# One-slot tiles in strict turn for every ring of a gated recurrence with a feed-forward network

## The chip, the core and the metric

The kernel runs on one core of a Trainium2 chip. The metric is the time of one execution on the device in microseconds (us); lower is better. The core has five engines: PE (TensorE, the matrix engine), DVE (VectorE), ACT (ScalarE), POOL (GpSimd) and SP (SyncE, which here only issues DMAs). Each works through its own queue in order, and semaphores order them against each other. SBUF is the on-chip memory for data, PSUM the memory that PE writes to.

## The reference

A recurrence over time whose decay depends on a gate, and then a network of two products and two more matrix products, for 4 x 5824 = 23296 tokens of 256 channels:

```python
a_base = 1.0 / (1.0 + np.exp(-a_param))
sig_r = 1.0 / (1.0 + np.exp(-r_gate))
sig_i = 1.0 / (1.0 + np.exp(-i_gate))
log_a = 8.0 * sig_r * np.log(np.clip(a_base, 1e-06, 1.0 - 1e-06))[None, None, :]
a_t = np.exp(log_a)
norm = np.sqrt(np.maximum(1.0 - a_t * a_t, 1e-06))
x_gated = norm * sig_i * x
for t in range(S):
    h = a_t[:, t] * h + x_gated[:, t]
    y[:, t] = h
# then, with y as 23296 rows of 256:
a = y @ w1            # 256 -> 1024
b = y @ w2            # 256 -> 1024
h = a * b @ w3        # 1024 -> 1024
out = h @ w_out       # 1024 -> 256
```

## The kernel before

The tokens are cut into 47 chunks: two of 256, 44 of 512 and one of 256. For each chunk the kernel loads the two gates and x (`r`, `i`, `x`), takes tanh of the gates on ACT, multiplies the input gate with x on POOL or DVE, turns both products so that channels lie on partitions (on PE through PSUM for the first chunks, by a transposing DMA later), forms the decay with an exponential (ACT), its square (POOL, ACT or DVE) and its root (ACT), runs the recurrence as a scan on DVE (`h`), and casts it to bf16 (`y`, mostly POOL). PE then multiplies with w1 (`a` steps, tiles `pa`) and w2 (`b` steps, tiles `pb`); ACT or DVE copies `pa` to SBUF (`c` steps, tiles `sa`); DVE multiplies that copy with `pb` (`m` steps, tiles `g_t`); PE multiplies with the product of w3 and w_out (`D` steps, tiles `po`), ACT or DVE copies that to SBUF (`e` steps, tiles `ot`), and SP stores it (`o` steps). The product of w3 and w_out is formed once in the first 50 us (`Ft`, `Fc`, `Fm`, `Fe` steps, after the loads `L` and casts `C` of the weights).

The order of the work is written out by hand: the string ORDER is a list of some two thousand words, one a step, and the scheduler keeps that order on every engine (`tc.manual_schedule()`, L76; the loop at L570 to L572). In a word the first number is the chunk. `a0.3.1` is the product with w1 for chunk 0, pair 3, half 1; `c0.3.1` is the copy of its result; `b1.2` is the product with w2 for chunk 1, pair 2; `m1.2` multiplies the two; `V4` turns the recurrence gate of chunk 4 and `U4` its gated input; `d4.0` is the decay of chunk 4 for the first half of the channels, `h` the scan, `y` the cast. `W` steps are matmuls without use that keep PE busy in the first microseconds.

Tiles come from pools. A pool with `bufs=N` has N slots for each tag (or as many as the call's own `bufs` says), and tiles of one tag share them. When the program is compiled, each tile is given one of the slots of its tag that are free at that point of the scheduler's own order of events; the choice is then fixed in the program as an address. At run time the first instruction that writes a tile waits, by semaphore, for the last instruction that used the tile before it in the same slot. That wait is in the engine's queue, and what stands behind it in the queue waits too. I call the first write of a new tile a take, and the end of the last use of a tile its release.

The rings are: in PSUM `po` (4 slots of one bank, shared by the tiles `pa`, `po`, `ptr`, `ptw` and `pw`) and `pb` (2 slots of two banks, shared by `pb`, the warm-up tiles and one small one); in SBUF `r` 4, `i` 5, `x` 4, `th_r` 2, `u` 2, `rt` 2, `ut` 6, `a` 6, `nrm` 6 (the last two shared with the staged weights), `h` 2, `y` 4, `sa` 3, `g` 3, `ot` 3, `w3` 4 and `w3t` 2. In the compiled program before, 499 tiles go through the `po` ring and 188 through `sa`.

The lines of the pools are L55 to L62; every helper that takes a tile does so in one line, such as L264 in `up_a` or L281 in `copy`. The instructions of matmuls with w1 and w2 all stand at L260, of `D` steps at L299, copies at L274 (DVE) and L276 (ACT), casts of `y` at L250, scans at L241, products at L288.

Of the kernel before, what the change touches and what calls it, by code (L numbers as in the profile page):

```python
# [22 lines left out]
def kernel(  # L23
# [13 lines left out]
    P = 128  # L37
# [15 lines left out]
    starts = [sum(sizes[:c]) for c in range(NCH)]  # L53

    consts = ctx.enter_context(tc.tile_pool(name="consts", bufs=1))  # L55
    loads = ctx.enter_context(tc.tile_pool(name="loads", bufs=3))
    gates = ctx.enter_context(tc.tile_pool(name="gates", bufs=2))
    held = ctx.enter_context(tc.tile_pool(name="held", bufs=6))
    ypool = ctx.enter_context(tc.tile_pool(name="ypool", bufs=2))
    ffn = ctx.enter_context(tc.tile_pool(name="ffn", bufs=3))  # L60
    psum_b = ctx.enter_context(tc.tile_pool(name="psum_b", bufs=2, space=bass.MemoryType.PSUM))
    psum_o = ctx.enter_context(tc.tile_pool(name="psum_o", bufs=4, space=bass.MemoryType.PSUM))  # L62

    ident_f = consts.tile([P, P], F32, tag="ident_f")
    make_identity(nc, ident_f)
# [29 lines left out]
    FOLD_ACT = {('c', 7), ('e', 0), ('e', 1), ('e', 2), ('e', 3), ('e', 7)}  # L95
    W_ACT = {('w2', 0), ('w3', 6)}
    W_DVE = {('w1', 1)}
    LOAD_BUFS = {"r": 4, "i": 5, "x": 4}
    STAGE = {'w1': ['a', 'a'], 'w2': ['nrm', 'nrm'], 'wo': ['a', 'nrm'], 'w3': ['a', 'nrm', 'a', 'nrm', 'a', 'nrm',
        'a', 'nrm']}  # L100
    CASTING = set()
    WARM = [8, 8, 8, 8, 8, 8, 8, 8, 8, 8, 8, 8, 8, 8, 8, 8]
    src = {"r": rf, "i": jf, "x": xf}

    def flat(t):
# [18 lines left out]

    def load(c, nm):
        n = sizes[c] // P
        t = loads.tile([P, 4, D], F32, name=nm + "_t", tag=nm, bufs=LOAD_BUFS[nm])
        nc.sync.dma_start(  # L128
            out=t[:, :n, :],
            in_=src[nm][starts[c]:starts[c] + sizes[c], :].rearrange("(p n) c -> p n c" if long_rows(c) else "(n p) c -> p n c", p=P))  # L130
        T[nm, c] = t

    def tanh_r(c):
        n = sizes[c] // P
        t = gates.tile([P, NCB, 4, P], BF16, name="th_r", tag="th_r")
        if c in TURN_R:
            nc.scalar.activation(out=flat(t)[:, :n, :], in_=T["r", c][:, :n, :], func=AF.Tanh, scale=0.5)
        else:
            nc.scalar.activation(out=dense(t, n).rearrange("p cb j q -> p j cb q"), in_=cut(T["r", c])[:, :n],  # L139
                                 func=AF.Tanh, scale=0.5)  # L140
        T["thr", c] = t
# [11 lines left out]
    def times(c, half):  # L153
        n = sizes[c] // P
        fused = c in DV_TIMES
        if half == 0 or fused:
            T["u", c] = gates.tile([P, NCB, 4, P], BF16, name="u_t", tag="u")
        u, t, xt = T["u", c], T["thi", c], T["x", c]
        js = slice(0, n) if fused else slice(half * n // 2, (half + 1) * n // 2)
        if c in TURN_U:  # L160
            u, t, xt = flat(u)[:, js, :], t[:, js, :], xt[:, js, :]
        else:
            u, t, xt = dense(u, n).rearrange("p cb j q -> p j cb q")[:, js], cut(t)[:, js], cut(xt)[:, js]
        if fused:
            parts = [slice(None)] if c in TURN_U else [(slice(None), slice(None), cb) for cb in range(NCB)]
            for part in parts:
                nc.vector.scalar_tensor_tensor(out=u[part], in0=t[part], scalar=1.0, in1=xt[part],
                                               op0=ALU.add, op1=ALU.mult)
        else:
            (nc.vector if (c, half) in DV_HALF else nc.gpsimd).tensor_mul(out=u, in0=t, in1=xt)  # L170

    def turn_pe(c, key, nm):
        n = sizes[c] // P
        pt = psum_o.tile([P, NCB, CT], BF16, name="ptr", tag="po")
        for cb in range(NCB):
            for j in range(n):
                nc.tensor.matmul(  # L177
                    out=pt[:, cb, j * P:(j + 1) * P],
                    lhsT=flat(T[nm, c])[:, j, cb * P:(cb + 1) * P], rhs=ident,
                    is_transpose=True,  # L180
                    start=(cb == 0 and j == 0), stop=(cb == NCB - 1 and j == n - 1))
        T[key, c] = pt

    def turn_dma(c, key, nm):
        pool, tag = (gates, "rt") if key == "pr" else (held, "ut")
        dst = pool.tile([P, NCB, 4, P], BF16, name=tag, tag=tag)
        n = sizes[c] // P
        nc.sync.dma_start_transpose(out=dense(dst, n).rearrange("p cb j q -> p (cb j) q"),
                                    in_=dense(T[nm, c], n).rearrange("p cb j q -> p (cb j q)"))
        T[key, c] = dense(dst, n).rearrange("p cb j q -> p cb (j q)")  # L190

    def decay(c, cb):
        w = sizes[c]
        if cb == 0:
            T["a", c] = held.tile([P, NCB, CT], F32, name="a_t", tag="a")
        a, pr = T["a", c][:, cb, :w], T["pr", c][:, cb, :w]
        if long_rows(c):
            a, pr = in_time(a), turned(pr)
        nc.scalar.activation(out=a, in_=pr, func=AF.Exp, scale=la4[:, cb:cb + 1], bias=la4[:, cb:cb + 1])  # L199

    def square(c, cb):
        w = sizes[c]
        if cb == 0:
            T["n", c] = held.tile([P, NCB, CT], F32, name="nrm", tag="nrm")
        n, a = T["n", c][:, cb, :w], T["a", c][:, cb, :w]
        if (c, cb) in AC_SQUARE:
            nc.scalar.activation(out=n, in_=a, func=AF.Square)
# [20 lines left out]
    def scan(c, cb):  # L228
        w = sizes[c]
        if cb == 0:  # L230
            T["h", c] = ypool.tile([P, NCB, CT], F32, name="h_t", tag="h")
        h, a, n = (T[key, c][:, :, :w] for key in "han")
        if cb == 0:
            for b in range(1, B):
# [7 lines left out]

    def cast(c):
        w = sizes[c]
        T["y", c] = ypool.tile([P, NCB, CT], BF16, name="y_t", tag="y", bufs=4)
        if c in AC_CAST:
            nc.scalar.copy(out=T["y", c][:, :, :w], in_=T["h", c][:, :, :w])
        else:
# [1 line left out]
            eng.tensor_copy(out=T["y", c][:, :, :w], in_=T["h", c][:, :, :w])  # L250

    def warm(i):
        pp = psum_b.tile([P, 2, CT], F32, name="warm", tag="pb")
        for _ in range(WARM[i]):
            nc.tensor.matmul(out=pp[:, 0, :P], lhsT=ident, rhs=ident, start=True, stop=True)  # L255

# [4 lines left out]
                             rhs=T["y", c][:, cb, :w], start=(cb == 0), stop=(cb == NCB - 1))  # L261

    def up_a(c, mp, q):
        T["pa", c, mp, q] = pp = psum_o.tile([P, CT], F32, name="pa", tag="po")  # L264
        up(c, 2 * mp + q, pp, w1_sb)

    def up_b(c, mp):
        T["pb", c, mp] = pp = psum_b.tile([P, 2, CT], F32, name="pb", tag="pb")
        for q in range(2):
            up(c, 2 * mp + q, pp[:, q, :], w2_sb)  # L270

# [6 lines left out]
    def copy(c, mp, q):  # L278
        w = sizes[c]
        if q == 0:  # L280
            T["sa", c, mp] = ffn.tile([P, 2, CT], BF16, name="sa", tag="sa")  # L281
        copy_to((c, mp, q) in DV_COPY, T["sa", c, mp][:, q, :w], T["pa", c, mp, q][:, :w])

    def product(c, mp):
        w = sizes[c]
        if mp == 0:
            T["g", c] = ffn.tile([P, KD, CT], BF16, name="g_t", tag="g")
        nc.vector.tensor_mul(out=T["g", c][:, 2 * mp:2 * mp + 2, :w], in0=T["sa", c, mp][:, :, :w],  # L288
                             in1=T["pb", c, mp][:, :, :w])

    def down(c, j):
        if c == NCH - 1:
            T["po_last", j] = po = psum_o.tile([P, D], F32, name="po", tag="po")
        else:
            if j % 2 == 0:
                T["po", c, j // 2] = psum_o.tile([P, 2, D], F32, name="po", tag="po")
            po = T["po", c, j // 2][:, j % 2, :]
        for k in range(KD):
            nc.tensor.matmul(out=po,  # L299
# [1 line left out]
                             start=(k == 0), stop=(k == KD - 1), skip_group_check=True)  # L301

    def evac(c, j2):
        T["ot", c, j2] = ffn.tile([P, 2, D], F32, name="ot", tag="ot")
        copy_to((c, j2) in DV_EVAC, T["ot", c, j2], T["po", c, j2])

    def evac_last(c, j):
        if j % 2 == 0:
            T["ot", c, j // 2] = ffn.tile([P, 2, D], F32, name="ot", tag="ot")
        copy_to(j % 2 == 0, T["ot", c, j // 2][:, j % 2, :], T["po_last", j])  # L310

    def store_last(c, j):
# [24 lines left out]
    def load_w(nm, i):  # L337
        if (nm, i) in CASTING:
            dst = piece(nm, i)[1]
            if dst is None:  # L340
                T["w3b", i] = dst = ffn.tile([P, 1, DFF], BF16, name="w3_t", tag="w3", bufs=4)
            nc.gpsimd.dma_start(out=dst, in_=piece(nm, i)[0])
            return
        T["wf", nm, i] = held.tile([P, NCB, CT], F32, name="wf", tag=STAGE[nm][i])
        nc.sync.dma_start(out=staged(nm, i), in_=piece(nm, i)[0])

    def cast_w(nm, i):
        dst = piece(nm, i)[1]
        if dst is None:
            T["w3b", i] = dst = ffn.tile([P, 1, DFF], BF16, name="w3_t", tag="w3", bufs=4)  # L350
        if (nm, i) in W_ACT:
            nc.scalar.copy(out=dst, in_=staged(nm, i))
        else:
            (nc.vector if (nm, i) in W_DVE else nc.gpsimd).tensor_copy(out=dst, in_=staged(nm, i))

    def fold_t(mi):
        pt = psum_o.tile([P, KD, P], BF16, name="ptw", tag="po")
        for k in range(KD):
            nc.tensor.matmul(out=pt[:, k, :], lhsT=T["w3b", mi][:, 0, k * P:(k + 1) * P], rhs=ident,  # L359
                             is_transpose=True, start=(k == 0), stop=(k == KD - 1))  # L360
        T["ptw", mi] = pt

    def fold_c(mi):
        T["w3t", mi] = ffn.tile([P, KD, P], BF16, name="w3t", tag="w3t", bufs=2)
        copy_to(("c", mi) not in FOLD_ACT, T["w3t", mi], T["ptw", mi])

    def fold_m(mi):
        po = psum_o.tile([P, D], F32, name="pw", tag="po")
        for k in range(KD):
            nc.tensor.matmul(out=po, lhsT=T["w3t", mi][:, k, :], rhs=wo_sb[:, k, :],  # L370
                             start=(k == 0), stop=(k == KD - 1))
# [3 lines left out]
        nc.vector.tensor_copy(out=ident, in_=ident_f)  # L375

    def rates_turn():
        pt = psum_b.tile([P, 2, CT], F32, name="pr_la", tag="pb")
        nc.tensor.matmul(out=pt[:, 0, :NCB], lhsT=la_rows, rhs=ident_f[:NCB, :NCB], is_transpose=True,
                         start=True, stop=True)  # L380
        T["la"] = pt[:, 0, :NCB]
# [219 lines left out]
```

## Time and profile before

| what | value |
|---|---|
| time, median of 3 runs | 519.78 us (519.36 to 521.22) |
| span of the profiled execution | 518.3 us |
| granted clock of TensorE, mean | 0.993 |
| HBM read, written | 78.91 MB, 23.86 MB |
| costliest chain lines | PE L299 28%, PE `pb` L260 28%, PE `pa` L260 27% |

The profile is one execution. Busy shares are of the whole span. "PEclk" is the TensorE clock that was granted, in tenths, in 40 equal slices of the span (13 us each). The chain of waits is followed back from the last instruction; its shares say on which engine the time was spent that set the end. In a timeline a row gives the start in us, the duration in us, the engine, the line, the operation, the tile written and the tiles read, and in brackets how long the engine was idle before it and what ended that. A table of waits gives, for each waiting instruction and each releaser, the total in us, the number of times and the longest.

### The profile page before, as it was taken

The page shows a single profiled execution, that of the slowest core. Times are in us where ns is not written, and L with a number is a line of the kernel's source. Part 1 is how long each engine was busy: PE and PEld are TensorE (multiplying, and loading weights), DVE is VectorE, ACT ScalarE, POOL GpSimd, SP SyncE. Part 2 cuts the span into 40 slices and gives each one's busy share as a digit, 9 for nine tenths or more (in the row PEclk, how much of TensorE's full clock was granted, in tenths as well). Part 3 has the DMA queues.
Part 4 walks back from the last instruction along what each step waited for, and adds up shares of the span by engine and source line. Part 5 has one row for each costly group of instructions (what it writes and reads, how often), then busy time and mean ns, then how long its engine had stood idle before and what let it go on. Part 6 is the DMA issues. An engine that isn't in the chain of part 4 may idle for free.

```text
span 518.3 us, 9099 instructions
## 1 busy us (share of the span) xinstructions
PE 505.2 (97%) x3321; PEld 316.1 (61%) x3321; DVE 428.8 (83%) x414; ACT 466.4 (90%) x720; POOL 314.3 (61%) x271
## 2 busy tenths in 40 slices
PE   7889999999999999999999999999999999999997
PEld 6748665566565566656666656564665665656566
DVE  5869999899899979878879889878888697859762
ACT  7969999999899999999999999998999879888543
POOL 1674657666636975785594985857756659480200
PEclk9979999999999999999999999999999999999999
DMA  8996999989999998998999976989794996352112
GB/s 293 409 414 224 274 341 261 284 260 291 334 232 234 286 266 270 245 214 236 321 296 272 320 231 182 246 224 270 178 277 118 229 290 194 102 144 80 51 62 103
DMA packets 177282, 123.82 MB, mean 239 GB/s; under 512 B 86354, under 2 KB 172884, under 8 KB 177236
## 3 DMA queue, kind: packets, MB, share of 16 engines
q1 hardware_dynamic: 177232, 123.23, 84.2%
q8 instruction: 26, 0.43, 0.3%
q14 instruction: 20, 0.16, 0.1%
q10 hardware_dynamic: 4, 0.00, 0.0%
HBM read 78.91 MB, written 23.86 MB: 198 GB/s over the span
## 4 chain that ended last, share of the span: by engine, by line
PE 85%; DVE 7%; ACT 2%; issue 2%; DMA 2%; SPq 1%; DVEq 0%; ACTq 0%
PE po L299 28%; PE pb L260 28%; PE pa L260 27%; DVE g_t L288 2%; DVE h_t L241 2%; DMA r_t<-in_r_gate_dram 2%; PE pw L370 1%; DVE nrm L224 1%; PE ptr L177 1%; DVE sa L274 1%; PE ptw L359 1%; ACT sa L276 1%; SPq L128 1%; ACT a_t L199 0%; ACT i_t L146 0%
## 5 line engine op out<-in xcount | busy, mean ns | idle before, releaser
L288 DVE TENSOR_TENSOR g_t<-sa,pb 128x1024 bf16<-128x1024 bf16 (+1 forms) x188 | 218.8, 1180 | 65.3 <-PE pb L260 33.0
L260 PEld LDWEIGHTS <-w_sb 128*128 128x128 bf16 x1504 | 147.3, 98 | 150.2 <-issue 9.3
L276 ACT CAST sa<-pa 128x512 bf16<-128x512 f32 (+1 forms) x339 | 182.5, 587 | 29.8 <-PE pa L260 23.2
L260 PE MATMUL pa<-y_t,w_sb 128*128 128x512 bf16 (+1 forms) x752 | 192.2, 374 | 5.8 <-DVE sa L274 4.5
L260 PE MATMUL pb<-y_t,w_sb 128*128 128x512 bf16 (+1 forms) x752 | 185.8, 374 | 0.0
L299 PE MATMUL po<-wp_sb,g_t 128*128 128x256 bf16 x1456 | 177.7, 273 | 0.0
L299 PEld LDWEIGHTS <-g_t 128*128 128x128 bf16 x1456 | 142.4, 98 | 40.0 <-issue 0.2
L250 POOL CAST y_t<-h_t 128x1024 bf16<-128x1024 f32 (+1 forms) x46 | 51.1, 1112 | 141.1 <-DVE h_t L241 134.6
L170 POOL TENSOR_TENSOR u_t<-i_t,x_t 128x512 bf16<-128x512 f32 (+1 forms) x89 | 121.2, 1378 | 5.8 <-DMA ut<-u_t 3.3
L241 DVE TENSOR_TENSOR_SCAN h_t<-a_t,h_t,nrm 128x512 f32<-128x512 f32 (+1 forms) x92 | 120.1, 1335 | 1.9
L209 POOL TENSOR_TENSOR nrm<-a_t 128x512 f32<-128x512 f32 (+1 forms) x74 | 80.9, 1111 | 15.0 <-ACT a_t L199 14.2
L151 POOL TENSOR_SCALAR i_t<-i_t 128x1024 f32<-128x1024 f32 (+1 forms) x45 | 53.7, 1195 | 19.5 <-ACT i_t L146 19.5
L199 ACT ACTIVATE a_t<-rt,la 128x512 f32<-128x512 bf16 (+1 forms) x80 | 64.1, 819 | 0.0
L276 ACT COPY ot<-po 128x512 f32<-128x512 f32 (+1 forms) x85 | 49.6, 589 | 13.1 <-PE po L299 12.2
L224 DVE SCALAR_TENSOR_TENSOR nrm<-nrm,ut 128x1024 f32<-128x1024 f32 (+1 forms) x39 | 53.5, 1373 | 6.4 <-ACT nrm L213 6.4
L146 ACT ACTIVATE i_t<-i_t 128x1024 f32<-128x1024 f32 (+1 forms) x47 | 49.0, 1045 | 0.3 <-DMA i_t<-in_i_gate_dram 0.3
L213 ACT ACTIVATE nrm<-nrm 128x1024 f32<-128x1024 f32 (+1 forms) x47 | 48.4, 1041 | 0.2
L139 ACT ACTIVATE th_r<-r_t 128x1024 bf16<-128x1024 f32 (+1 forms) x40 | 42.5, 1063 | 0.0
L274 DVE CAST sa<-pa 128x512 bf16<-128x512 f32 (+1 forms) x37 | 21.9, 615 | 3.1 <-PE pa L260 2.9
L213 ACT ACT_TABLE_LOAD x17 | 21.8, 1283 | 0.3
L199 ACT ACTIVATE a_t<-ptr,la 128x512 f32<-128x512 bf16 (+1 forms) x14 | 9.6, 712 | 1.4 <-POOL nrm L209 1.3
L255 PE MATMUL warm<-ident 128*128 128x128 bf16 x128 | 10.7, 253 | 0.0
(57 smaller groups left out, 134.8 us busy)
## 6 DMA issues: line engine op xcount, KB each, us to landing
out_dram<-ot SPq DMA_DIRECT2D x90, 256.0 KB, 3.5
r_t<-in_r_gate_dram SPq DMA_DIRECT2D x44, 512.0 KB, 5.5
i_t<-in_i_gate_dram SPq DMA_DIRECT2D x44, 512.0 KB, 6.2
x_t<-in_x_dram SPq DMA_DIRECT2D x44, 512.0 KB, 5.6
wf<-in_moe_w_dram SPq DMA_DIRECT2D x12, 512.0 KB, 10.2
wf<-in_moe_w_out_dram SPq DMA_DIRECT2D x2, 512.0 KB, 10.3
r_t<-in_r_gate_dram SPq DMA_DIRECT2D x3, 256.0 KB, 3.0
i_t<-in_i_gate_dram SPq DMA_DIRECT2D x3, 256.0 KB, 4.3
```

Of the source, the lines that this page charges most:

```text
L151: (nc.vector if c in DV_PLUS else nc.gpsimd).tensor_scalar(t, t, 1.0, 1.0, op0=ALU.add, op1=ALU.mult)
L170: (nc.vector if (c, half) in DV_HALF else nc.gpsimd).tensor_mul(out=u, in0=t, in1=xt)
L199: nc.scalar.activation(out=a, in_=pr, func=AF.Exp, scale=la4[:, cb:cb + 1], bias=la4[:, cb:cb + 1])
L209: (nc.vector if (c, cb) in DV_SQUARE else nc.gpsimd).tensor_mul(out=n, in0=a, in1=a)
L213: nc.scalar.activation(out=T["n", c][:, :, :w], in_=T["n", c][:, :, :w], func=AF.Sqrt, scale=-1.0, bias=1.0)
L224: nc.vector.scalar_tensor_tensor(out=T["n", c][:, :, :w], in0=T["n", c][:, :, :w], scalar=1e-3, in1=T["pu", c][:, :, :w], op0=ALU.max, op1 ...
L241: nc.vector.tensor_tensor_scan(h[:, cb, :], a[:, cb, :], n[:, cb, :], init, ALU.mult, ALU.add)
L250: eng.tensor_copy(out=T["y", c][:, :, :w], in_=T["h", c][:, :, :w])
L260: nc.tensor.matmul(out=dst[:, :w], lhsT=w_sb[:, cb, m * P:(m + 1) * P], rhs=T["y", c][:, cb, :w], start=(cb == 0), stop=(cb == NCB - 1))
L276: nc.scalar.copy(out=dst, in_=src_ps)
L288: nc.vector.tensor_mul(out=T["g", c][:, 2 * mp:2 * mp + 2, :w], in0=T["sa", c, mp][:, :, :w], in1=T["pb", c, mp][:, :, :w])
L299: nc.tensor.matmul(out=po, lhsT=T["g", c][:, k, j * P:(j + 1) * P], rhs=wp_sb[:, k, :], start=(k == 0), stop=(k == KD - 1), skip_group_che ...
```

## The change

All pools get `bufs=1`, and each ring is made of tags of its own with one slot each, `po_0` to `po_3` for `po` and so on. A helper `ring` counts the takes of each ring in the order in which ORDER makes them and hands out the slots strictly in turn: take k goes into slot k mod N. The number of slots, their sizes, the instructions, the engines and ORDER are the same.

```diff
-    loads = ctx.enter_context(tc.tile_pool(name="loads", bufs=3))
-    gates = ctx.enter_context(tc.tile_pool(name="gates", bufs=2))
...
-    psum_b = ctx.enter_context(tc.tile_pool(name="psum_b", bufs=2, space=bass.MemoryType.PSUM))
-    psum_o = ctx.enter_context(tc.tile_pool(name="psum_o", bufs=4, space=bass.MemoryType.PSUM))
+    loads = ctx.enter_context(tc.tile_pool(name="loads", bufs=1))
+    gates = ctx.enter_context(tc.tile_pool(name="gates", bufs=1))
...
+    psum_b = ctx.enter_context(tc.tile_pool(name="psum_b", bufs=1, space=bass.MemoryType.PSUM))
+    psum_o = ctx.enter_context(tc.tile_pool(name="psum_o", bufs=1, space=bass.MemoryType.PSUM))
...
-    LOAD_BUFS = {"r": 4, "i": 5, "x": 4}
...
+    RINGS = {"r": 4, "i": 5, "x": 4, "th_r": 2, "u": 2, "rt": 2, "ut": 6, "a": 6, "nrm": 6, "h": 2, "y": 4,
+             "sa": 3, "g": 3, "ot": 3, "w3": 4, "w3t": 2, "po": 4, "pb": 2}
+    taken = dict.fromkeys(RINGS, 0)
+
+    def ring(pool, shape, dtype, name, tag):
+        slot = taken[tag] % RINGS[tag]
+        taken[tag] += 1
+        return pool.tile(shape, dtype, name=name, tag=f"{tag}_{slot}")
+
...
-        T["pa", c, mp, q] = pp = psum_o.tile([P, CT], F32, name="pa", tag="po")
+        T["pa", c, mp, q] = pp = ring(psum_o, [P, CT], F32, name="pa", tag="po")
...
-            T["sa", c, mp] = ffn.tile([P, 2, CT], BF16, name="sa", tag="sa")
+            T["sa", c, mp] = ring(ffn, [P, 2, CT], BF16, name="sa", tag="sa")
```

The other helpers that take a tile are changed in the same way.

More of the change, by code (lines that the diff above doesn't have):

```diff
@@ L55 @@
     consts = ctx.enter_context(tc.tile_pool(name="consts", bufs=1))
-    loads = ctx.enter_context(tc.tile_pool(name="loads", bufs=3))
-    gates = ctx.enter_context(tc.tile_pool(name="gates", bufs=2))
-    held = ctx.enter_context(tc.tile_pool(name="held", bufs=6))
-    ypool = ctx.enter_context(tc.tile_pool(name="ypool", bufs=2))
-    ffn = ctx.enter_context(tc.tile_pool(name="ffn", bufs=3))
-    psum_b = ctx.enter_context(tc.tile_pool(name="psum_b", bufs=2, space=bass.MemoryType.PSUM))
-    psum_o = ctx.enter_context(tc.tile_pool(name="psum_o", bufs=4, space=bass.MemoryType.PSUM))
+    loads = ctx.enter_context(tc.tile_pool(name="loads", bufs=1))
+    gates = ctx.enter_context(tc.tile_pool(name="gates", bufs=1))
+    held = ctx.enter_context(tc.tile_pool(name="held", bufs=1))
+    ypool = ctx.enter_context(tc.tile_pool(name="ypool", bufs=1))
+    ffn = ctx.enter_context(tc.tile_pool(name="ffn", bufs=1))
+    psum_b = ctx.enter_context(tc.tile_pool(name="psum_b", bufs=1, space=bass.MemoryType.PSUM))
+    psum_o = ctx.enter_context(tc.tile_pool(name="psum_o", bufs=1, space=bass.MemoryType.PSUM))
     ident_f = consts.tile([P, P], F32, tag="ident_f")
@@ L126, in load @@
         n = sizes[c] // P
-        t = loads.tile([P, 4, D], F32, name=nm + "_t", tag=nm, bufs=LOAD_BUFS[nm])
+        t = ring(loads, [P, 4, D], F32, name=nm + "_t", tag=nm)
         nc.sync.dma_start(
@@ L134, in tanh_r @@
         n = sizes[c] // P
-        t = gates.tile([P, NCB, 4, P], BF16, name="th_r", tag="th_r")
+        t = ring(gates, [P, NCB, 4, P], BF16, name="th_r", tag="th_r")
         if c in TURN_R:
@@ L156, in times @@
         if half == 0 or fused:
-            T["u", c] = gates.tile([P, NCB, 4, P], BF16, name="u_t", tag="u")
+            T["u", c] = ring(gates, [P, NCB, 4, P], BF16, name="u_t", tag="u")
         u, t, xt = T["u", c], T["thi", c], T["x", c]
@@ L173, in turn_pe @@
         n = sizes[c] // P
-        pt = psum_o.tile([P, NCB, CT], BF16, name="ptr", tag="po")
+        pt = ring(psum_o, [P, NCB, CT], BF16, name="ptr", tag="po")
         for cb in range(NCB):
@@ L185, in turn_dma @@
         pool, tag = (gates, "rt") if key == "pr" else (held, "ut")
-        dst = pool.tile([P, NCB, 4, P], BF16, name=tag, tag=tag)
+        dst = ring(pool, [P, NCB, 4, P], BF16, name=tag, tag=tag)
         n = sizes[c] // P
@@ L194, in decay @@
         if cb == 0:
-            T["a", c] = held.tile([P, NCB, CT], F32, name="a_t", tag="a")
+            T["a", c] = ring(held, [P, NCB, CT], F32, name="a_t", tag="a")
         a, pr = T["a", c][:, cb, :w], T["pr", c][:, cb, :w]
@@ L203, in square @@
         if cb == 0:
-            T["n", c] = held.tile([P, NCB, CT], F32, name="nrm", tag="nrm")
+            T["n", c] = ring(held, [P, NCB, CT], F32, name="nrm", tag="nrm")
         n, a = T["n", c][:, cb, :w], T["a", c][:, cb, :w]
@@ L230, in scan @@
         if cb == 0:
-            T["h", c] = ypool.tile([P, NCB, CT], F32, name="h_t", tag="h")
+            T["h", c] = ring(ypool, [P, NCB, CT], F32, name="h_t", tag="h")
         h, a, n = (T[key, c][:, :, :w] for key in "han")
@@ L244, in cast @@
         w = sizes[c]
-        T["y", c] = ypool.tile([P, NCB, CT], BF16, name="y_t", tag="y", bufs=4)
+        T["y", c] = ring(ypool, [P, NCB, CT], BF16, name="y_t", tag="y")
         if c in AC_CAST:
@@ L252, in warm @@
     def warm(i):
-        pp = psum_b.tile([P, 2, CT], F32, name="warm", tag="pb")
+        pp = ring(psum_b, [P, 2, CT], F32, name="warm", tag="pb")
         for _ in range(WARM[i]):
@@ L263, in up_a @@
     def up_a(c, mp, q):
-        T["pa", c, mp, q] = pp = psum_o.tile([P, CT], F32, name="pa", tag="po")
+        T["pa", c, mp, q] = pp = ring(psum_o, [P, CT], F32, name="pa", tag="po")
         up(c, 2 * mp + q, pp, w1_sb)
     def up_b(c, mp):
-        T["pb", c, mp] = pp = psum_b.tile([P, 2, CT], F32, name="pb", tag="pb")
+        T["pb", c, mp] = pp = ring(psum_b, [P, 2, CT], F32, name="pb", tag="pb")
         for q in range(2):
@@ L286, in product @@
         if mp == 0:
-            T["g", c] = ffn.tile([P, KD, CT], BF16, name="g_t", tag="g")
+            T["g", c] = ring(ffn, [P, KD, CT], BF16, name="g_t", tag="g")
         nc.vector.tensor_mul(out=T["g", c][:, 2 * mp:2 * mp + 2, :w], in0=T["sa", c, mp][:, :, :w],
@@ L292, in down @@
         if c == NCH - 1:
-            T["po_last", j] = po = psum_o.tile([P, D], F32, name="po", tag="po")
+            T["po_last", j] = po = ring(psum_o, [P, D], F32, name="po", tag="po")
         else:
             if j % 2 == 0:
-                T["po", c, j // 2] = psum_o.tile([P, 2, D], F32, name="po", tag="po")
+                T["po", c, j // 2] = ring(psum_o, [P, 2, D], F32, name="po", tag="po")
             po = T["po", c, j // 2][:, j % 2, :]
@@ L303, in evac @@
     def evac(c, j2):
-        T["ot", c, j2] = ffn.tile([P, 2, D], F32, name="ot", tag="ot")
+        T["ot", c, j2] = ring(ffn, [P, 2, D], F32, name="ot", tag="ot")
         copy_to((c, j2) in DV_EVAC, T["ot", c, j2], T["po", c, j2])
@@ L308, in evac_last @@
         if j % 2 == 0:
-            T["ot", c, j // 2] = ffn.tile([P, 2, D], F32, name="ot", tag="ot")
+            T["ot", c, j // 2] = ring(ffn, [P, 2, D], F32, name="ot", tag="ot")
         copy_to(j % 2 == 0, T["ot", c, j // 2][:, j % 2, :], T["po_last", j])
@@ L340, in load_w @@
             if dst is None:
-                T["w3b", i] = dst = ffn.tile([P, 1, DFF], BF16, name="w3_t", tag="w3", bufs=4)
+                T["w3b", i] = dst = ring(ffn, [P, 1, DFF], BF16, name="w3_t", tag="w3")
             nc.gpsimd.dma_start(out=dst, in_=piece(nm, i)[0])
             return
-        T["wf", nm, i] = held.tile([P, NCB, CT], F32, name="wf", tag=STAGE[nm][i])
+        T["wf", nm, i] = ring(held, [P, NCB, CT], F32, name="wf", tag=STAGE[nm][i])
         nc.sync.dma_start(out=staged(nm, i), in_=piece(nm, i)[0])
@@ L349, in cast_w @@
         if dst is None:
-            T["w3b", i] = dst = ffn.tile([P, 1, DFF], BF16, name="w3_t", tag="w3", bufs=4)
+            T["w3b", i] = dst = ring(ffn, [P, 1, DFF], BF16, name="w3_t", tag="w3")
         if (nm, i) in W_ACT:
@@ L356, in fold_t @@
     def fold_t(mi):
-        pt = psum_o.tile([P, KD, P], BF16, name="ptw", tag="po")
+        pt = ring(psum_o, [P, KD, P], BF16, name="ptw", tag="po")
         for k in range(KD):
@@ L363, in fold_c @@
     def fold_c(mi):
-        T["w3t", mi] = ffn.tile([P, KD, P], BF16, name="w3t", tag="w3t", bufs=2)
+        T["w3t", mi] = ring(ffn, [P, KD, P], BF16, name="w3t", tag="w3t")
         copy_to(("c", mi) not in FOLD_ACT, T["w3t", mi], T["ptw", mi])
     def fold_m(mi):
-        po = psum_o.tile([P, D], F32, name="pw", tag="po")
+        po = ring(psum_o, [P, D], F32, name="pw", tag="po")
         for k in range(KD):
@@ L377, in rates_turn @@
     def rates_turn():
-        pt = psum_b.tile([P, 2, CT], F32, name="pr_la", tag="pb")
+        pt = ring(psum_b, [P, 2, CT], F32, name="pr_la", tag="pb")
         nc.tensor.matmul(out=pt[:, 0, :NCB], lhsT=la_rows, rhs=ident_f[:NCB, :NCB], is_transpose=True,
```

## The prediction

> **What bounds the kernel now.** First the page, for who is busy and for the chain that ended last.
>
> ```profile
> PE 505.2 (97%) x3321; PEld 316.1 (61%) x3321; DVE 428.8 (83%) x414; ACT 466.4 (90%) x720; POOL 314.3 (61%) x271
> PEclk9979999999999999999999999999999999999999
> PE 85%; DVE 7%; ACT 2%; issue 2%; DMA 2%; SPq 1%; DVEq 0%; ACTq 0%
> ```
>
> TensorE is the bound, and the chain agrees. The one dip of its clock is in the third slice. Next I asked for the waits of PE alone, the only idle time that can be won directly.
>
> ```profile
> PE pa L260 <- DVE sa L274: 4.5, 3, 3.1
> PE pr_la L379 <- DMA la_rows<-in_a_param_dram: 2.1, 1, 2.1
> PE ptr L177 <- ACT th_r L137: 1.8, 2, 1.5
> PE pa L260 <- ACT sa L276: 0.8, 1, 0.8
> PE pa L260 <- POOL y_t L250: 0.3, 1, 0.3
> PE pa L260 <- DVE ot L274: 0.2, 1, 0.2
> ```
>
> Rows 2 and 3 are the first inputs and no slot's. The first row is the `po` ring: a take of a PSUM tile waits for the copy that frees a slot. Its longest wait, 3.1 us, stands in the timeline of 24.2 to 29.5 us.
>
> ```profile
> 24.93 0.38 PE L260 MATMUL pa<-y_t,w_sb 128*128 128x256 bf16 x2
> 25.78 0.36 ACT L276 CAST sa<-pa 128x256 bf16<-128x256 f32 x1
> 27.91 0.42 DVE L274 CAST sa<-pa 128x256 bf16<-128x256 f32 x1
> 28.39 0.58 PE L260 MATMUL pa<-y_t,w_sb 128*128 128x256 bf16 x2 [3.07 <-DVE sa L274]
> ```
>
> The table of busy time by stage shows what follows it, and who else is full later (stretch; its length, then busy us of PE, PEld, DVE, ACT and POOL with counts; clock, DMA share, GB/s).
>
> ```profile
> 25.00:27.00 2.00, 0.31 (x3) 0.13 (x3) 2.00 (x2) 2.00 (x6) 0.00 (x0) 1.00 1.02 414
> 28.40:30.00 1.60, 1.60 (x8) 1.12 (x8) 0.00 (x0) 0.90 (x2) 1.60 (x2) 0.50 1.03 422
> 34.00:36.00 2.00, 2.00 (x12) 0.95 (x10) 1.38 (x2) 0.58 (x1) 1.92 (x2) 1.00 1.02 416
> 34.00:60.00 26.00, 26.00 (x226) 18.52 (x224) 23.54 (x31) 23.34 (x32) 13.47 (x13) 1.00 0.80 268
> 80.00:100.00 20.00, 20.00 (x135) 12.38 (x134) 19.38 (x22) 19.91 (x29) 13.35 (x13) 1.00 1.12 274
> ```
>
> After the wait PE runs at half clock; the clock's record has 0.5 from 27.0 to 33.8 us. From 34 us on PE has hardly a gap; from 60 us on ScalarE is full too (19.91 of 20).
>
> **What the Trainium skill says.** "TensorE: Matmul & The Clock Gate", section "What's actually happening", says that an idle window of about 3.4 us halves the clock, and that the window runs free. The trace agrees in kind: clock 0.50 after the wait. It shows the drop a little sooner, 1.7 us into the wait, so the wait need not fill a window. "PSUM — Partial Sum Buffer", section "Engine vs sequencer instructions": matmuls start and complete in program order, and ScalarE's and VectorE's queues are strictly first in, first out. The trace agrees: for 3.07 us nothing behind the take starts. "Perfetto Trace Analysis", section "Optimization Strategy": the same gap coming again and again can mean too few buffers. Here it doesn't come again: PE's waits on a `po` slot are a handful.
>
> **The change part by part.** The number of slots of each ring, the instructions and their order on each queue (SP's and POOL's included) stay: no instruction is added, removed or moved. What changes is which earlier tile a new one follows into its slot, so which last reader its first writer waits for. Before, the slots fixed in the compiled program are not in turn: in `po` 215 of 499 tiles do not follow the tile 4 takes back (109 of them would have a later release in turn, 106 an earlier one), in `sa` 67 of 188, in `r`, `i`, `a`, `nrm`, `ot` some 22 to 28 each, in `h` and `w3t` none. To price it I wrote out each ring's takes in the order of ORDER and put the start of each take's first writer beside the end of the last reader N takes back, both from the timeline of before.
>
> (1) *The wait at 25.3 us.* The take is `a0.3.1`. Before, it follows `a1.2.0` two takes back, whose reader is the DVE cast that ends at 27.91 + 0.42 = 28.33. In turn it follows `a1.3.1`, whose ACT cast ends at 25.78 + 0.36 = 26.14. PE is free at 25.31, so the wait shrinks from 3.07 to about 0.9: 2.2 us. With a gap of 0.9 (one of 0.83 at 17.8 us left the clock at full) I take the drop to stay away: PE is busy from 28.39 to 33.83 at half clock, so half of 5.4, 2.7, is won too. Sum 4.9, if the others follow. Followed by hand: after `a0.3.1` PE has b1.2, a1.2.1, V4 and b0.3, about 1.7 us at full clock, which ends near 28.4; a2.0.0 needs y2, whose POOL cast ends at 27.29 + 1.04 = 28.33 and doesn't move. DVE then does c1.2.1 (0.42), m1.2 (0.69), m0.3 (0.69) from 28.35, to 30.15, which frees the `pb` slot of b2.0: 30.3, against a row of 34.51 before. So 4.2. From there to 47 us ACT waited for PE 2.6 + 1.0 us (`sa`, `w3t`) and 1.3 for a row that ends with PE's V4; DVE 2.7 + 1.1 + 0.4. These waits are where both catch up. The loads read from 43 to 57 us, which DMA paces and which don't move, land 6.3 us or more before their first reader. I take 4.0.
>
> (2) *Other waits on `po`.* At 102.0 us PE waits 1.24 for a DVE cast; in turn the slot is free at 100.24 + 0.57 = 100.81, before PE comes. In turn two takes at 88.4 and 94.1 us would wait 0.10 and 0.22; with 0.05 each from release to start, 0.42. Net 0.8 won at most; with ACT full there (19.9 of 20) it may be waited for again. I take half: 0.4.
>
> (3) *Takes that get a wait.* Of 495 takes of `po`, eight began before their turn's release: by 0.22 (18.6 us), 0.10, 0.22 (both counted), 0.25 (135.4), 0.14, 0.34 (144.9), 0.02 and 0.29 (377.5): 1.58 in all. What is queued behind each is every later matmul, and ACT and DVE wait for those. The first lies ahead of the shortened wait. The three at 135 to 145 us (0.73, and 0.05 each: 0.9) stand beside waits of before in 134 to 154 us (0.19, 0.27 and 0.24) which they in part replace: 0.3 lost. The last two: 0.4 lost.
>
> (4) *SBUF rings.* `sa`: seven takes, 2.55 us in all, the longest 0.93 at 396.5 on ACT, where ACT has idle time (47.42 of 50 busy in 350 to 400 us); one ACT wait of 1.54 at 133 us goes. `g` 0.66, `w3` 0.32 on DVE and POOL, which are not full there. On SP: `i` 1.47 (67.6 us) and 2.22 (277.8), `r` 0.83 (181.8) and 2.63 (291.5), `rt` 1.65 (351.1); behind these stand the next loads, transposes and stores of SP. Their leads from landing to first read are 4.2 us or more at the first four places, and 2.2 for the transpose held 1.65. Hidden: 0. Bounds: a gain of 1.5 (ACT's wait) and a loss of 1.5.
>
> Sum: -4.0 - 0.4 + 0.3 + 0.4 = -3.7, against the profiled span of 518.3: 514.6. The timed runs stood at a median of 519.78, 1.5 above that span, so 516.1.
>
> **The rivals.** *(A) The forecast*, 516.1, own range 514.2 to 517.1. *(B) The start is won and given back*: with ACT full from 60 us on, PE's lead is waited off wherever in-turn slack is short, or the clock still drops for part of the 6.8 us. For it: takes of `po` with under 0.5 us of slack go from 49 to 88. Against it: ACT's own idle time in 28 to 47 us lets it move along. Half the gain left: about 518.2. *(C) Slower*: one slow reader now blocks the whole ring. Place: `po` in 60 to 350 us, where ACT is full. In turn 51 takes there have under 0.5 us of slack, 27 before. If ACT releases half a microsecond later against PE than in this trace, the 24 more takes wait some 0.25 each, 6.0, and (2) and (3) turn to +2: 519.78 - 4.0 + 6.0 + 2.0 = 523.8. It decides once ACT lags by 0.5; ACT waits for PE 36 times in `sa` alone, which speaks against. *(D) More*: the start gives its whole 4.9, 102 us its 0.8, and ACT the 1.5: 512.9. *That the change does nothing* is excluded: the slots differ in 215 places.
>
> **How the numbers follow.** A 0.58, B 0.23, C 0.14, D 0.05. Two measurements of this kernel can't tell less than about 0.5%, 2.6 us. Faster is A and D, 0.63; B is same, 0.23; slower 0.14. The range takes in A, nearly all of B and the bounds of (4): 513.6 to 520.4.
>
> **What would show it.** After: no PE wait over 1.5 us after 20 us; clock at 1.0 from about 10 us on; b2.0 near 30.3 and chunk 7's work some 4 us earlier; small waits of `pa` and `po` on ACT in 88 to 145 us, 0.3 or less each. I'm wrong if the clock still drops, if PE's waits for ACT exceed 2 us in 60 to 350 us, or if SP's held loads show as waits of ACT on DMA.

## The result and the profile after

| | median | lowest to highest | ratio to before, 95% interval |
|---|---|---|---|
| before, same chip | 519.83 us | 519.31 to 522.07 | |
| after | 516.40 us | 514.88 to 518.02 | 0.9926 [0.9897, 0.9955] |

The changed kernel is 3.4 us faster, where 3.7 was forecast; the interval excludes no change, but its upper end, 0.9955, falls just short of the half per cent that the forecast took as the least that can be told. The profiled execution has a span of 513.8 us against 518.3.

The page after, in the order in which the page before was read: busy time by engine, the granted clock in 40 slices, the chain that ended last.

```profile
PE 499.8 (97%) x3267; PEld 314.2 (61%) x3321; DVE 430.6 (84%) x414; ACT 465.5 (91%) x720; POOL 312.9 (61%) x271
PEclk9999999999999999999999999999999999999999
PE 86%; ACT 5%; DMA 4%; issue 2%; DVE 2%; SPq 1%; ACTq 0%; DVEq 0%
```

PE is still the bound. Its busy time can't be set against that of before, because the records of 54 of 3321 matmuls are missing here (x3267); the weight loads are all there, so I follow those. The dip in the third slice is gone: in this execution the clock stays at full from 8.7 us on. The waits of PE:

```profile
PE pa L268 <- ACT sa L284: 3.5, 3, 2.2
PE ptr L185 <- ACT th_r L145: 2.2, 2, 1.2
PE pr_la L387 <- DMA la_rows<-in_a_param_dram: 2.1, 1, 2.1
PE pw L378 <- POOL wo_sb L362: 0.2, 1, 0.2
```

The wait of 3.1 us for DVE has become one of 2.2 for ACT. It shrank by 0.9, not by the 2.2 of the forecast. The timeline of 24.2 to 31 us shows it (start, duration, engine, line, what; in brackets the idle time before it and what ended that):

```profile
24.37 1.28 ACT L145 ACT_TABLE_LOAD   x1 [1.18 <-DMA r_t<-in_r_gate_dram]
...
25.13 0.38 PE L268 MATMUL pa<-y_t,w_sb 128*128 128x256 bf16 x2
...
25.67 1.06 ACT L145 ACTIVATE th_r<-r_t 128x1024 bf16<-128x1024 f32 x1
...
27.29 0.36 ACT L284 CAST sa<-pa 128x256 bf16<-128x256 f32 x1
...
27.70 0.38 PE L268 MATMUL pa<-y_t,w_sb 128*128 128x256 bf16 x2 [2.19 <-ACT sa L284]
```

The take `a0.3.1` now waits for the ACT copy `c1.3.1`, as forecast. But that copy ends at 27.65, where before it ended at 26.14, mostly because ACT sat idle for 1.18 us ahead of its table load, waiting for the load of `r` of chunk 4 (the other 0.3 us were lost in ACT's queue earlier). The same stretch of ACT's queue before the change has no such idle time:

```profile
22.86 1.28 ACT L137 ACT_TABLE_LOAD   x1
24.16 1.06 ACT L137 ACTIVATE th_r<-r_t 128x1024 bf16<-128x1024 f32 x1
25.12 0.76 ACT L199 ACTIVATE a_t<-ptr,la 128x512 f32<-128x512 bf16 x1
25.78 0.36 ACT L276 CAST sa<-pa 128x256 bf16<-128x256 f32 x1
```

Busy time by stage after (stretch, length, busy us of PE, PEld, DVE, ACT, POOL with counts; clock, DMA share, GB/s):

```profile
25.00:34.00 9.00, 6.75 (x53) 4.33 (x53) 7.33 (x12) 8.99 (x16) 6.42 (x7) 1.00 1.03 417
34.00:60.00 26.00, 25.84 (x220) 18.57 (x221) 24.50 (x31) 24.92 (x35) 16.78 (x16) 1.00 0.91 310
80.00:100.00 20.00, 19.81 (x124) 11.77 (x126) 19.30 (x22) 19.91 (x30) 13.25 (x13) 1.00 1.12 277
```

The clock is 1.00 in all three. In 34 to 60 us ACT is busy for 24.92 us where it had 23.34, and DVE for 24.50 instead of 23.54: they have moved along with PE. From 34 to 350 us PE has no listed wait at all.

Where the time came from is seen best by matching the weight loads of the two traces one to one and taking the start after from the start before. I call that the lead (the column head is the time before; a column with a range of times gives the rounded value in it):

| at, us | 23 | 28.4 | 30 | 33 | 34 to 88 | 95 to 101 | 102 | 105 to 134 | 154 to 200 | 205 to 348 | 378 to end |
|---|---|---|---|---|---|---|---|---|---|---|---|
| lead of PE, us | -0.20 | 0.68 | 1.34 | 2.64 | 3.24 | 2.97 | 4.38 | 4.2 | 5.24 | 4.81 | 4.48 |

ACT and DVE show nearly the same lead (ACT 3.24 at 51 to 103 us, later 5.24, 4.81 and 4.48): they go in step with PE. Only at 134 us is ACT further ahead, by 5.72. So the start is worth 3.4 (from -0.20 to 3.24), the stretch from 88 to 105 us about 0.9 (1.4 at the wait at 102 us, less three small losses beside it), the stretch from 135 to 154 us about 1, and some 0.8 is given back later.

### The profile page after: what moved, and what is told of

The parts are those of the page before. It is cut to its first block, busy times and chain, and to the rows that moved or that the text cites. A ratio compares the mean times of both kernels' runs of the same rounds, so it can differ in the third digit from the quotient of the medians.

```text
span 513.8 us, 9036 instructions
## 1 busy us (share of the span) xinstructions
PE 499.8 (97%) x3267; PEld 314.2 (61%) x3321; DVE 430.6 (84%) x414; ACT 465.5 (91%) x720; POOL 312.9 (61%) x271
## 4 chain that ended last, share of the span: by engine, by line
PE 86%; ACT 5%; DMA 4%; issue 2%; DVE 2%; SPq 1%; ACTq 0%; DVEq 0%
PE po L307 29%; PE pb L268 28%; PE pa L268 27%; DMA r_t<-in_r_gate_dram 4%; ACT sa L284 2%; PE pw L378 1%; PE ptr L185 1%; DVE g_t L296 1%; PE ptw L367 1%; ACT ot L284 1%; SPq L136 1%; DVE h_t L249 1%; ACT i_t L154 1%; ACT a_t L207 1%; ACT L154 0%
## 5 line engine op out<-in xcount | busy, mean ns | idle before, releaser
L284 ACT CAST sa<-pa 128x512 bf16<-128x512 f32 (+1 forms) x339 | 182.4, 588 | 27.6 <-PE pa L268 18.3
L268 PE MATMUL pa<-y_t,w_sb 128*128 128x512 bf16 (+1 forms) x721 | 185.9, 372 | 4.5 <-ACT sa L284 3.5
L268 PE MATMUL pb<-y_t,w_sb 128*128 128x512 bf16 (+1 forms) x729 | 182.5, 372 | 1.5
L178 POOL TENSOR_TENSOR u_t<-i_t,x_t 128x512 bf16<-128x512 f32 (+1 forms) x89 | 120.0, 1365 | 5.5 <-DMA ut<-u_t 2.5
L215 ACT ACTIVATE nrm<-a_t 128x512 f32<-128x512 f32 (+1 forms) x17 | 10.7, 648 | 0.1
## 6 DMA issues: line engine op xcount, KB each, us to landing
wf<-in_moe_w_out_dram SPq DMA_DIRECT2D x2, 512.0 KB, 10.5
```

The source lines that it names most:

```text
L268: nc.tensor.matmul(out=dst[:, :w], lhsT=w_sb[:, cb, m * P:(m + 1) * P], rhs=T["y", c][:, cb, :w], start=(cb == 0), stop=(cb == NCB - 1))
L284: nc.scalar.copy(out=dst, in_=src_ps)
```

## The experiments

The forecast's theory was: the gain lies in the `po` ring, most of it in the one take at 25 us and the clock behind it; the SBUF rings bring nothing. The rivals: the gain is in later takes, or SBUF rings take part of it back. After the result there was a second question: what held the start at 3.4 and the wait at 2.19.

Most kernels below are the changed kernel with a table that gives a ring the slots that it had in the compiled program of before, one digit a take (shortened here):

```diff
+    SLOTS = {"pb": "0101...", "sa": "0121...", ...}
     def ring(pool, shape, dtype, name, tag):
-        slot = taken[tag] % RINGS[tag]
+        slot = int(SLOTS[tag][taken[tag]]) if tag in SLOTS else taken[tag] % RINGS[tag]
```

A ring that is not in the table takes its slots in turn. With all rings in it, every wait of the compiled program is that of before. So what differs below is the order of the slots; that each slot is a tag of its own changes no wait.

### Only `po` in turn

The table holds every ring except `po`.

> Only the PSUM ring of the a, D, V, U, Ft and Fm steps (po) is taken in turn; every other ring has the slots of before. Theory (the gain is PE's waits on po, the one at 25 us above all): as the changed kernel, 515.5 to 517.5 us, PE ahead by about 3 us at 40 us. Rival (the gain comes from the SBUF rings, whose waits sit on ACT, DVE, POOL and SP): 518.5 to 520.

Measured: 515.98 us (515.50 to 517.28), ratio 0.9932 [0.9915, 0.9948], mean clock 0.999 or more in each of the six runs. The timeline at the take:

```profile
23.13 1.28 ACT L169 ACT_TABLE_LOAD   x1
...
26.11 0.36 ACT L308 CAST sa<-pa 128x256 bf16<-128x256 f32 x1
...
26.52 0.38 PE L292 MATMUL pa<-y_t,w_sb 128*128 128x256 bf16 x2 [0.82 <-ACT sa L308]
```

Here the wait is 0.82, the 0.9 of the forecast, and the copy ends at 26.47. The lead is 3.81 at 37 to 86 us, 4.93 at 102, 3.99 after 135, 4.29 at 148 and 4.04 from 389 us on. So `po` alone brings the whole gain, and with `po` alone the start comes out as it was worked out (4.0). Something in the other rings makes the wait longer.

### Only the SBUF rings in turn

The table holds `po` and `pb` alone.

> The reverse: po and pb have the slots of before, all SBUF rings are taken in turn. Theory: 519 to 520.5 us, with the 3 us wait at 25 us and the half clock after it still there. Rival (SBUF rings): 516 to 517.5.

Measured: 519.10 us (518.01 to 520.85), ratio 0.9991 [0.9981, 1.0]. The waits of PE have the old row at the old size:

```profile
PE pa L279 <- DVE sa L293: 4.6, 3, 3.1
```

The half clock is still there, from 27.6 to 34.4 us. The lead is -0.33 after the start and +0.40 later. The SBUF rings bring next to nothing by themselves, within what the measurement can tell from no change. (`pb`, the other PSUM ring, has the slots of before in this kernel and in the last one; it was not tried by itself.)

### Only the start, and only the rest

In the first, the first 63 takes of `po` go in turn and the later ones follow the order of before; all other rings are as before. In the second, the first 63 takes of `po` have the slots of before and all else is in turn.

> po is taken in turn for its first 63 takes (to about 62 us), and has the order of slots of before from then on; all other rings as before. Theory (most of the gain is made at 25 us): 516 to 517.5 us, PE ahead by 3.2 us at 40 us and by no more at the end. Rival (the gain is the sum of many later takes): 519 to 520.

> The reverse: the first 63 takes of po have the slots of before, everything else is in turn. Theory: the wait at 25 us stays, later waits on po at 102 and near 145 us shrink by about 1 us each and some 0.8 is lost to new ones after 190 us, so 518 to 519.5 us. Rival (many later takes): 516 to 517.5.

The start alone: 516.65 us (515.88 to 516.95), 0.9937 [0.9921, 0.9954]; clock 0.999 or more in all six. The rest alone: 518.20 us (517.41 to 519.48), 0.9975 [0.9962, 0.9987]. PE's waits, first of the start alone:

```profile
PE pa L298 <- ACT sa L314: 2.0, 2, 1.1
...
PE pa L298 <- DVE sa L312: 1.4, 2, 1.2
```

And those of the rest alone:

```profile
PE pa L276 <- DVE sa L290: 3.1, 1, 3.1
...
PE pa L276 <- ACT sa L292: 1.0, 2, 0.8
```

The start alone loses the 3.1 us row and keeps the 1.2 of 102 us; the rest alone does the opposite. The lead of the start alone is 3.68 from 35 to 260 us and 3.37 at the end: won once and kept. The lead of the rest alone must be read with care: its profiled execution had half clock only from 28.3 to 31.7 us, and so starts with 0.82 that no slot brought. From there it goes to 1.94 at 102 us, 1.73 at 132, 2.63 at 163 to 193 and 1.85 from 389: 1.0 net for the later takes. By medians the rest alone stands 0.9 below the SBUF rings alone (518.20 against 519.10), which agrees, though fewer of its runs have the longer half clock that is counted below (3 of 13 against 8 of 22).

### What the half clock costs by itself

All rings as before, so the take waits as before. But PE gets 20 matmuls without use, ahead of `a1.2.0`; they fill most of the time in which it would wait. They write the unused half of the bank that holds `pw`, and the output is the same.

```diff
-        po = ring(psum_o, [P, D], F32, name="pw", tag="po")
+        both = ring(psum_o, [P, 2, D], F32, name="pw", tag="po")
+        po = both[:, 0, :]
...
+        if mi == 2:
+            for _ in range(20):
+                nc.tensor.matmul(out=both[:, 1, :], lhsT=ident, rhs=wo_sb[:, 0, :], start=True, stop=True)
```

> The slots of before in every ring, with 20 matmuls of 128x256 added after those of Fm2, into the unused half of that bank, so that PE is busy for 2.2 us of the 3.1 us wait, which otherwise stays: PE gets no work done earlier. Theory (a large part of the gain is the half clock after the wait): clock 1.0, 517.5 to 518.5 us. Rival (only the wait counts): 519.5 to 520.5.

Measured: 517.87 us (517.32 to 518.37), ratio 0.9969 [0.9956, 0.9981]; mean clock 1.0 in all eight runs.

```profile
24.95 2.35 PE L414 MATMUL pw<-wo_sb,ident 128*128 128x256 bf16 x20
...
27.13 0.38 PE L298 MATMUL pa<-y_t,w_sb 128*128 128x256 bf16 x2
...
28.40 0.38 PE L298 MATMUL pa<-y_t,w_sb 128*128 128x256 bf16 x2 [0.89 <-DVE sa L312]
```

The take starts at 28.40, before at 28.39: not a tenth of a microsecond of the wait is won, only the clock, and that is worth 1.6 us (0.31%). The runs of the kernel before, taken beside these experiments, say the same when they are sorted by mean clock. In the clock's records the half clock lasts 3.4 us (rest alone) or 6.8 us (before, SBUF rings alone). I call 3.4 us a stretch. One stretch lowers the mean over 518 us by 1.7/518, to 0.997; two lower it to 0.993.

| stretches at half clock | none | one | two |
|---|---|---|---|
| runs of before | 8 | 48 | 10 |
| median, us | 517.96 | 519.59 | 520.86 |

So the usual run of before loses 1.6 us to the clock. The profiled execution, on which the 2.7 us of the forecast rest, is one of those with two stretches.

### What makes the take wait 2.19 us

In the compiled programs, the ACT instructions ahead of `c1.3.1` differ in one thing:

```
before:  table load | th_r, waits for r of chunk 4 | wait: DMA | a_t, waits for PE
after:   wait: r of chunk 4 | table load | th_r, waits for PE | a_t, waits for DMA
```

The tile is `th_r` of chunk 4, in a ring of two slots; ORDER takes them for chunks 1, 0, 3, 2 and 4. Before, chunk 4's followed chunk 2's into its slot, and needed no wait of its own for that. In turn it follows chunk 3's, and has to wait for PE, which reads that tile in `V3`. It already had a wait for its load. In these programs an instruction that computes carries one wait; here the second becomes an instruction of its own, and it stands ahead of the table load. Before, the 1.28 us of the table load (22.86 to 24.14 us) ran while the load of `r` was on its way (it lands at 24.07); after, it can only begin when `r` has landed (at 24.30). First test: the changed kernel with the slots of before for `th_r` alone.

```diff
+    SLOTS = {"th_r": "01011010101010101010101010101010010101101010101"}
```

> The changed kernel, but the ring th_r has the slots of before. In turn, the tanh of chunk 4 has to wait for a second engine, and the compiler puts its wait for the load of r4 into an instruction of its own ahead of the 1.28 us table load, which then no longer hides behind that load. Theory: this put about 1.2 us on ACT's copy c1.3.1, for which PE's take at 25 us waits, so here PE's wait is 0.7 to 1.2 us instead of 2.2, the clock stays full in all runs, and the time is 515 to 515.8 us. Rival (the difference was chance of the loads): as the changed kernel, 516 to 517.

Measured: 515.10 us (514.38 to 516.84), ratio 0.9919 [0.9900, 0.9937]; clock 0.999 or more in all six.

```profile
23.45 1.28 ACT L148 ACT_TABLE_LOAD   x1
24.75 1.06 ACT L148 ACTIVATE th_r<-r_t 128x1024 bf16<-128x1024 f32 x1
...
26.37 0.36 ACT L287 CAST sa<-pa 128x256 bf16<-128x256 f32 x1
26.79 0.38 PE L271 MATMUL pa<-y_t,w_sb 128*128 128x256 bf16 x2 [1.18 <-ACT sa L287]
```

No idle time is left ahead of the table load, though `r` lands no earlier (at 24.36), and the take waits 1.18 instead of 2.19. The lead is 3.90 at 35 to 81 us, 5.03 at 102, 5.88 at 162 to 343 and 5.48 at the end: 1.0 more than after.

The rival was that the place of the copy in ACT's queue matters: moved ahead of `R4`, it would free the slot before the table load. It is tried with `th_r` in turn, and then together with the slots of before for `th_r`.

```diff
...
-  m1.1 c1.3.0 Fm2 R4 g2 h2.0 h2.1 d3.0 Lw3.7 c1.3.1 m0.2
+  m1.1 c1.3.0 Fm2 c1.3.1 R4 g2 h2.0 h2.1 d3.0 Lw3.7 m0.2
...
```

> The changed kernel with one word of ORDER moved: the copy c1.3.1 stands before the tanh R4 on ACT, so that the take at 25 us follows a copy that ends near 23.5. Theory: no PE wait there, clock full, 514 to 515.5 us, bounded by the cast y2 at 28.4. Rival (R4 and all behind it 0.4 later on ACT takes it back): 516 to 517.

> Both edits: th_r with the slots of before and c1.3.1 ahead of R4. Theory: at least as fast as either, 514 to 515.3 us; the th_r edit adds little once PE no longer waits behind R4. Rival: they add up, 513.5 or less.

The copy first: 516.71 us (514.98 to 517.38), 0.9938 [0.9918, 0.9958]. Both: 515.02 us (514.44 to 515.72), 0.9914 [0.9896, 0.9932]. The copy first:

```profile
25.19 0.37 ACT L286 CAST sa<-pa 128x256 bf16<-128x256 f32 x1 [1.06 <-PE ptr L187]
25.58 1.28 ACT L147 ACT_TABLE_LOAD   x1
...
26.81 0.61 PE L270 MATMUL pa<-y_t,w_sb 128*128 128x256 bf16 x4
...
27.84 1.43 ACT L209 ACTIVATE a_t<-ptr,la 128x512 f32<-128x512 bf16 x2
...
29.32 0.38 PE L270 MATMUL pa<-y_t,w_sb 128*128 128x256 bf16 x2 [1.46 <-ACT a_t L209]
```

The copy now stands ahead of the table load, and PE goes through both takes at 26.81; but the next one waits 1.46 us for ACT's decay, which the late table load still holds up. The wait has moved one take on: the forecast of no wait and 514 to 515.5 us was missed, and its rival's 516 to 517 came out. With `th_r` as before, the place of the copy changes nothing: 515.02 against 515.10.

The changed kernel and the one with the slots of before for `th_r` differ by little, so both were run once more, side by side on one chip.

> The changed kernel itself, beside the next one on the same chip. Theory (in turn th_r puts ACT's 1.28 us table load behind the load of r4): about 1 us slower than the next, 516 to 517, with half of its runs at a mean clock under 0.999. Rival (the two differ only by chance): the medians within 0.5 us of each other.

> The changed kernel with the slots of before for th_r alone, as run before. Theory: 515 to 515.8 us, mean clock 0.999 or 1.0 in every run. Rival: as the changed kernel beside it.

The changed kernel: 516.93 us (515.07 to 518.14), 0.9950 [0.9934, 0.9965]. With `th_r` as before: 514.87 us (514.66 to 515.98), 0.9921 [0.9902, 0.9941]. Side by side, `th_r` in turn costs 2.1 us. Against the runs of the changed kernel without a half clock it is 0.6 (515.48); the rest is the half clock. The changed kernel's profile this time holds a half clock (start of ACT's table load, then the wait, then the busy time by stage):

```profile
24.95 1.28 ACT L145 ACT_TABLE_LOAD   x1 [1.82 <-DMA r_t<-in_r_gate_dram]
...
28.28 0.38 PE L268 MATMUL pa<-y_t,w_sb 128*128 128x256 bf16 x2 [2.18 <-ACT sa L284]
```

```profile
27.00:30.50 3.50, 2.22 (x20) 1.85 (x20) 3.10 (x5) 3.50 (x8) 2.43 (x3) 0.87 1.02 412
30.50:34.00 3.50, 3.50 (x15) 1.67 (x14) 1.43 (x4) 2.76 (x5) 3.42 (x4) 0.64 1.03 421
```

A clock of 0.87 and 0.64 over 3.5 us each is 2 x (0.13 + 0.36) x 3.5 = 3.4 us at half clock: one stretch. Of the 13 runs of the changed kernel here, five have none (median 515.48 us) and eight have it (517.32 for the seven at 0.997); of the six of the first measurement three have it. Where the profile shows that take to wait 0.82 (only `po` in turn) or 1.1 to 1.2 us (`th_r` as before), none of 18 runs has one; with the copy first, where a take waits 1.46, three of six have, and with both edits (1.46) none of four. The longer wait is what brings the half clock back; at 1.46 us the runs are too few to say.

The kernel with `th_r` as before is faster than both: 4.5 us below before (519.35 beside it) and 2.1 below the changed kernel.

## Why the prediction was right

The time, 516.1 against 516.4, and the sign came out. Of the four steps, the mechanism of the first is shown. That the number is so near is in part luck. Between the two profiles 4.5 us were won (518.3 to 513.8), not 3.7. But the profile of before has two stretches at half clock and its median run one, while the profile after has none and about half of its runs one; so the medians differ by less, 3.4.

**(1) The wait at 25.3 us: right in place and cause, mis-sized by something that step (4) left out.** `b2.0` starts at 31.27, where the forecast had 30.3 and the row of before 34.51: 3.24 won, not 4.2, nor the 4.0 taken. The step put the release at 26.14, the end of `c1.3.1` before, and so took it, without saying so, that ACT's queue ahead of that copy doesn't move. It moved, by 1.5 us, mostly because of `th_r`. (`a1.2.0` is the take just before `a0.3.1`, not two back as the step has it; its reading of the two releases holds.) With `po` alone in turn the wait is 0.82 and the lead 3.81: there the step holds as it was worked out. That ACT and DVE catch up, on which the step rested, is shown by their leads.

The clock's term, 2.7 us, was right for the profiled execution (two stretches: 520.86 - 517.96 = 2.9) but too large for the median run of before, which has one (1.6). And "the drop stays away" is right in only part of the runs: eight of 19. At equal clock the change brings 517.96 - 515.48 = 2.5 us without a half-clock stretch, and about 2.3 with one (519.59 against 517.32); these take runs of several chips together, and those of the chip of the last pair alone give 2.2 and 2.0. The rest of the 3.4 is that fewer runs have one. So the forecast put too much of its sum on the clock, and came out because other terms were undersized.

**(2) The wait at 102.0 us: undersized.** 0.4 was taken, on the ground that ACT is full there; about 0.9 came, a little more than the 0.8 called the most (1.4 at the wait; 0.15 and 0.12 lost at 88.4 and 94.1 us, the two places named, and 0.2 at 104). ACT at 19.91 us of 20 was not a limit that ate the gain: it had moved ahead together with PE, by 3.24 us up to this place.

**(3) Takes that get a wait: the sign was wrong at the first place, the size right at the second.** A loss of 0.3 was put at 135 to 145 us. With `po` alone in turn it is there: 0.73 at 135.4 us, and from 4.7 to 4.4 over the whole place. In the changed kernel the lead grows there by about 1, from 4.2 to 5.24; step (4) has why. At 377 us 0.4 was taken off and 0.33 is gone. A loss of some 0.4 near 200 us was not in the step. The slots alone don't bring it: in the second profile of the changed kernel, the same program, the lead stays at 2.51 from 157 to 343 us.

**(4) SBUF rings at nothing: right for their sum, not for their parts.** Alone they give 0.9991 [0.9981, 1.0]. But they hold a gain and a loss. The gain: the 1.54 us wait of ACT at 133 us, which the step named as the bound above, does count. The waits of 120 to 140 us show how, first ACT's before, then ACT's and PE's with `po` alone in turn:

```profile
ACT sa L276 <- DVE g_t L288: 1.5, 1, 1.5
...
ACT sa L308 <- DVE g_t L320: 1.8, 1, 1.8
...
PE pa L292 <- ACT sa L308: 0.9, 1, 0.9
```

With `po` alone in turn ACT still waits for its `sa` slot, and PE's in-turn take waits for ACT's copy. In the changed kernel, and with `th_r` as before, neither wait is left, and ACT's lead goes up by 1.7 us at 134 us. No run has the `sa` ring alone put back, so that it is this ring and no other is read from the traces and was not tried by itself. The loss: `th_r`, of which the step said nothing. It looked at how long each take would be held, and that take is held by nothing (PE's reading ends early); it costs because a second wait moves the first one ahead of the table load. "No instruction is added, removed or moved" holds for the work, not for the waits. With the slots of before for `th_r`, the kernel gains 2.1 us side by side. In the kernel with only the SBUF rings in turn this loss can't be seen, since the take at 25 us waits for DVE there anyway.

**The rivals.** (C), slower through in-turn takes behind ACT in 60 to 350 us, is out: PE has no listed wait in 34 to 350 us. (B), the start won and given back, is out as to the waiting off, since the start alone keeps 3.4 of its 3.7 to the end; but its second sentence, that the clock may still drop for a part, is what happens in 11 of 19 runs. (D), more, is near what the kernel with `th_r` as before reaches: 514.9, where 512.9 was worked out.

**The signs named ahead.** Two failed: a PE wait over 1.5 us stays after 20 us (2.19), and the clock still drops in many runs. Held loads of SP as waits of ACT on DMA in 60 to 350 us do not appear. The first wait of ACT on a DMA that matters is at 24 us, and no slot's.

The Trainium skill's "TensorE: Matmul & The Clock Gate", section "What's actually happening", on which the clock's term rested, says that an idle window of about 3.4 us halves the clock and that the window runs free. The traces agree on the length, and a free run fits them. The clock's records change only at whole multiples of 3.41 us from their first rise (in the profile of before full for 17.07 us, 5 of them, then half for 6.83, 2 of them), and the first rise comes at a different moment in each profile, from 7.7 to 10.5 us after the start. But the window need not be idle. In the profile of before the one ahead of the drop goes from 23.59 to 27.00 us, and PE is busy for 1.55 us of it. And 2.2 us of idle time are enough in 11 of 19 runs, while 0.8 to 1.2 us brought it on in none of 18. That the place of the wait in the window decides which run has it fits, but is not shown: PE's busy time in the window alone does not sort the profiles (1.48 us and no drop in the first of the changed kernel, 1.30 and a drop in its second, 1.55 and a drop before).

## What to carry to other kernels

When slots change, look at each new wait not only for how long it holds, but for what stands behind it if it becomes an instruction of its own: here ACT's table load, which ran beside a DMA before, ended up behind it. Take a clock loss that comes in some runs and not in others from many runs and not from the one profiled execution, since that one may be among the worst. And strict turn is no rule: here at least one ring is better off with the slot that was free before, so try a single ring where the first trace shows a wait that the working didn't have.

## What was not expected of the hardware

The clock's drop comes in whole stretches of 3.4 us and not in every run: the same program runs with none, one or two (8, 48 and 10 runs of before; 8 and 11 of after with none and one), for 517.96, 519.59 and 520.86 us with the slots of before. That step of 2.9 us from none to two is nearly as large as the effect of the change, and it goes away when the wait is short (mean clock 0.999 or more in all twelve runs of the kernel whose profiles show it at 1.1 to 1.2 us) or filled with useless matmuls (1.0 in all eight).

A full ACT (19.91 of 20 us busy in 80 to 100 us) did not keep an earlier lead from passing through: from 34 to 88 us it stays at 3.24 without loss.
